# Five engine lists re-ordered over later landings of four weight pieces

## The chip, the cores and the metric

The kernel runs on one core of a Trainium2 chip. A core has a matrix engine (PE in the profile; its weight loads are shown apart as PEld), a vector engine (DVE), an activation engine (ACT), a general engine (POOL) and a queue engine (SP); 16 DMA engines move data between the core's memory and the device's memory. The metric is the time of one execution in microseconds of device time. Before the change the median of three runs is 207.43 us, the lowest 206.64 and the highest 209.45.

## The reference

```python
# x: 8 batches, 8 heads, 512 tokens, 64 wide; state: 8, 8, 32, 64
scores  = x @ state^T / 8;  a  = softmax(scores);   xread = a @ state
scores2 = state @ x^T / 8;  a2 = softmax(scores2);  sread = a2 @ x
y = concat([xread, sread], axis=2)   -> (8 * 544, 512), heads side by side
h = y @ w_in                          # 512 x 2048
g = s * relu(h) ** 2 + b
out = g @ w_out                       # 2048 x 512, float32
```

## The kernel before

**The work.** Batch by batch, the scores of x against the state are computed transposed (`T`), exponentiated on ACT (`E`) and divided by their sums (`a4`). The state is multiplied into the first weight ahead of time: `M[b, c]` is state of batch b times column chunk c of w_in, so that the first layer is `h = M^T a4`. ACT takes relu out of PSUM into `g`, DVE squares it. The second layer for batches 1 to 7 works with sums of blocks (`pd` from g, `u` from w_out; seven products in place of eight), batch 0 with plain products. The state's own rows (`sr`) go through both layers last.

**The lists.** Every piece of work is an `op` with a number, given in the order in which the Python code makes them. `TURNS` (lines 17 to 74) holds, for each of the five engines, the order in which it issues its ops; it also decides which engine does an op that two engines could do. `Plan.order` walks through these lists with a table of estimated durations. Two things come out of its estimates: which of a tag's buffers an op's output gets, and how many filler matmuls (`fill`, on the zero tile `warm`, 256 columns) are put on PE ahead of an op that, by the estimate, would find PE idle before 20 us. A filler is an instruction like any other: once it is in the list, PE runs it whether or not it would have had to wait. The constants `lands` of an op give the time at which a DMA is taken to have landed; `dma_free["sw"]` is the time at which POOL's DMA queue is taken to begin.

**The start.** SP issues the eight fp32 pieces first: ops 0 to 3 are batch 0 of x (`x0_load`, lines 446 to 453), ops 4 to 7 the four 128-row pieces k = 0 to 3 of the first column chunk of w_in (`wf_load`, lines 482 to 489). ACT or DVE casts them to fp16: ops 22 to 25 for x, 26 to 29 for w_in. POOL loads the rest with the cast done by the DMA, in the order wi 2 (op 15), wi 3 (17), wi 1 (13), wo 0 (14), x of batch 1 (18), wo 1, 2, 3 (16, 19, 20), x of batch 2 (21), each 512 KB.

For batch 0 the ops that follow are: transposes of x on PE (33, 35, 37, 39), copied to `xT` by 34, 36, 38, 40; scores of the two head groups (41, 42), their exponentials (43, 44), their sums on PE (45, 46), logarithm (47, 50), exponential of its negative (48, 51) and product (49, 52). `M[0, 0]` is op 58 on PE, which reads all four cast pieces; 59 and 60 copy its halves out of PSUM. Ops 76, 83 and 67 make `M[0, 2]`, `M[0, 3]` and `M[0, 1]` from POOL's pieces wi 2, wi 3 and wi 1. These, like every score and M op, work on tiles of 64 x 32 of the array ("tiled"); the others use all of it ("full"). The first layer of batch 0 is ops 90, 91, 94, 95, 98, 99, 102, 103 (two matmuls each) and 106, 109, 112, 115 (four each): 32 matmuls of 512 columns. Op 123 is the first product of the second layer, and reads wo 0. Later ops named below: 698 and 820 load x of batches 6 and 7 on POOL's queue; 818, 819 and 940, 941 are the DMA transposes of them on SP's queue (`att_xT_dma`, line 712), 714 the one of batch 5's quotient (line 937), 821 batch 6's scores on PE.

Every matmul is issued by the helper at line 338, every copy and cast by that at line 429.

Of the kernel before, what the change touches and what calls it, by code (L numbers as in the profile page):

```python
# [15 lines left out]

TURNS = {
    "PE": """
        33 31 35 41 37 39 45 42 58 46 94 76 90 95 91 109 83 106 112 67 115 98 102-103 99 123 127 124 135 128
        136-137 56 125 138 131 197 195 132-133 129 126 130 199 79 143 139-140 151 141 152 142 134 203 153  # L20
        144 154-155 145 202 146 156 159-160 157 161 158 162 86 118 171 175 167 172 253 173 176 174 121 147
        177 247 178 244 168 61 169 250 148 70 235 232 149-150 64 81 170 163 241 238 164 183-184 165 340 73
        1061 185-186 166 179-180 343-344 181 268 182 277-278 269-271 279 272 280 273-274 281-282 275 361 349
        1066 283 352 355 358 287 284 288-289 455 88 364 290-292 296 293-294 297-298 370 299-303 305 464 706
        704 306 315 307-310 367 316-318 311-312 577 580 586 319-321 325 322 326-327 458 460 1071 328-332 462
        699 582 385-388 477 389 394 390 395 486 471 480 391 396 489 392 397-398 474 399-400 1076 401 404-405
        492 406-408 413 409-411 414-416 602 417 599 418-420 422-424 708 702 584 425-429 432 483 442-443 433
        444-445 434-435 611 436-437 446 614 447-449 438-439 605 608 596 507-511 516 512 517 724 518-519
        513-514 520-522 721 526 523 527-529 593 530-533 535-541 821 1086 1081 542 544-549 554-555 550-551
        942 945 949 556 564 557 565-569 558 570-571 733 736 559-561 718 638-639 730 629 640 630-634 727 641  # L30
        635-636 642-643 830 826 951 644-645 648-650 715 651 855 657 652-655 658-663 666-667 664 668-672
        676-677 673 678 1096 1091 858 679-683 686 828 947 824 751 687 752 688 753 689 754 690 837 755
        691-693 849 756 846 757 760-766 758 843 767 964 770-774 779 775 780-781 776-777 782-783 840 852
        784-785 788 786 789-793 798 794-795 967 799-804 808-809 805 810-811 979 812-814 973 976 873 815
        874-875 1106 876-877 961 882-883 878-879 884-885 880 886 1111 892 970 887-888 893-895 889 1101
        896-899 901-903 958 904-907 910 908 911-917 1116 920 930-932 921 933 1136 1131 934-936 922 937 1126
        923-926 994 927 995-1001 1003 1121 1004-1008 1013-1015 1009-1010 1016-1020 1022-1027 1031-1032
        1028-1029 1033-1037 1041 1038 1042-1046 1051 1047-1048 1052-1058 1153-1160 1162-1169 1172-1179
        1181-1188 1190-1197 1200-1207 1210-1217
    """,  # L40
    "ACT": """
        36 25 43 38 47 28 48 44 50-51 96 92 84 110 107 113 69 116 100 104 201 200 80 207-208 204-205 119 254
        248 245 63 251 71 236 233 82 66 242 239 342 341 75 345-346 362 350 353 356 359 457 456 89 365 371
        465 705 707 368 578-579 581 459 461 463 701 700 478 583 487 481 472 490 493 475 603 600 703 484 585
# [3 lines left out]
    """,  # L48
    "DVE": """
        22 30 23 34 32 24 27 26 40 29 59 53 49 60 52 77-78 85 1062 93 68 111 55 97 101 57 198 196 105 114  # L50
        108 117 11 209 226 206 10 228 87 220-221 120 122 216 187 189 217 219 62 246 249 230 72 335 255 252
        234 237 65 256-257 74 240 262 243 193 218 191 347 263-264 1067 1072 1063 229 224 1068 276 258-259
        265 260 225 222 354 266 285 360 267 295 227 357 261 366 304 467-468 223 469 313 587 351 231 376 323
        1073 1082 377 363 372 333 369 379 382 589 1077 373 380 590 374 591 393 378 383 402 491 375 482 479
        412 1078 421 498 381 476 430 711 384 494 712-713 473 499 604 450 485 440 488 601 504 495-496 607
        1087 598 515 505 501 610 502 524 616 500 534 613 595 497 543 1088 620 1083 503 552 621 626 506 617
        572 723 833 618 562 834 738 835 954 623-624 637 729 646 1097 619 622 627 735 720 656 628 1092 625
        955 665 732 717 726 674 745 1093 1098 684 739 956 748 740 742-743 749 694 851 741 839 746 759 744
# [5 lines left out]
    """,  # L64
    "POOL": """
        12 15 17 13-14 18 16 19-21 212 210 214 339 194 454 576 314 334 188 698 403 192 820 286 431 451 441
        190 525 324 1080 553 573 1065 1085 1100 1070 1095 769 685 1090 647 1075 695 797 563 675 939 929 919
        817 807 891
    """,
    "SP": """  # L70
        0-3 5 4 6-9 54 338 211 337 213 215 452 336 453 348 466 574-575 697 696 470 588 1064 592 710 818-819
        1079 714 940-941 1074 832 953 1089 1069 836 1094 1099 1084 957 1050 1060 1012 1171 1040 1199 1209
        1219
    """,
}

# [13 lines left out]
class Plan:  # L90
# [34 lines left out]
    def op(self, engs, fn, rd=(), wr=(), mode=None, dma=None, since=0.0, into=(), lands=None, mms=0):  # L125
        wr_all = [*wr, *((u,) for u in into)]
        o = Op(len(self.ops), engs, fn, rd, wr_all, mode, dma, since, lands, mms)
        for key in rd:
            o.before.update(self.wrote[key])
        for key in wr:  # L130
            o.before.update(self.wrote[key])
            o.before.update(self.read[key])
        for key in rd:
            self.read[key].append(o)
        for key in wr:
            self.wrote[key] = [o]
# [14 lines left out]
    def order(self, fill):  # L151
        free = {"PE": 2.88, "ACT": 2.4, "DVE": 1.3, "POOL": 0.5, "SP": 0.6}
        queue = {e: self.turns(e)[::-1] for e in free}
        assert sum(map(len, queue.values())) == len(self.ops)
        dma_free = {"sw": 8.6, "hw": 0.0}
        big, flying, weights = 0.0, [], []
        landed = {"sw": [], "hw": []}
        slot_free = {t: [0.0] * len(s) for t, s in self.slots.items()}
# [24 lines left out]
        while any(queue.values()):  # L183
# [27 lines left out]
            if e == "PE":  # L211
# [7 lines left out]
                if t < 20 and idle > 0.11 and spare:  # L219
                    tag, i = spare[0]  # L220
# [79 lines left out]
def kernel(  # L300
# [137 lines left out]
    def xf_ap(i):  # L438
        return plan.slots["u"][i // 2].bitcast(FP32).rearrange(
            "p (h f) -> p h f", h=4  # L440
        )[:, 2 * (i % 2) : 2 * (i % 2) + 2]

    def x0_heads(i):
        return slice(4 * (i % 2) + i // 2, 4 * (i % 2) + 4, 2)

    def x0_load(i):
        op(
            {"SP": 0.5},
            lambda e: nc.sync.dma_start(xf_ap(i), x0_v[:, x0_heads(i)]),  # L449
            wr=[K(("xf", i))],  # L450
            dma=("hw", 0.75),
            lands=(3.75, 4.7, 5.95, 6.25)[i],
        )

    def x0_cast(i):
# [35 lines left out]
    def wf_cast(k):  # L491
# [82 lines left out]
    for i in range(4):  # L574
        x0_load(i)
    for k in range(NKM):
        wf_load(k)
# [789 lines left out]
    for k in range(NKM):  # L1367
# [89 lines left out]
```

## Time and profile before

| what | value |
|---|---|
| median of the runs | 207.43 us (206.64 to 209.45) |
| the profiled execution, its own time | 207.94 us |
| its span, first to last instruction | 206.2 us |
| PE busy | 199.4 us, 97% of the span |
| DVE, ACT, POOL busy | 163.5, 111.9, 35.9 us |
| filler matmuls in PE's list | 49 of 256 columns, 4 of 512 |
| granted PE clock, mean | 1.00 |

Between the span and the execution's own time lie 1.7 us outside the program's instructions. A matmul's recorded duration overlaps the next one's: the pace is read from the starts of consecutive matmuls, or from a group's start and the start of what follows. A row of the timeline gives start, duration, engine, line, operation, output and inputs by tile name, shape and count, with the idle time before it and what ended it in brackets.

### The profile page before, as it was taken

Reading aid. Unit: us, or ns where it says so; the run is one execution under the profiler, and the core shown is the slowest. Engines: PE = TensorE matmul, PEld = TensorE weight load, DVE = VectorE, ACT = ScalarE, POOL = GpSimd, SP = SyncE. Lnnn points to the kernel's source line nnn. Section 1 sums busy time; section 2 is a strip of 40 time slices with the busy share of each in tenths; the row PEclk is TensorE's granted clock in tenths of the full one; section 3 lists DMA queues with packets and bytes.
Section 4 is the critical chain, followed back from the end, with each engine's and each line's share of the span. In section 5 each row is a group of like instructions: output and inputs, shape, how many; then the busy total and the mean of one; then the engine's idle time right before and its main releaser. Section 6 shows DMA issues by size and latency. Waiting matters only on the chain.

```text
span 206.2 us, 4764 instructions
## 1 busy us (share of the span) xinstructions
PE 199.4 (97%) x1979; PEld 134.1 (65%) x1979; DVE 163.5 (79%) x329; ACT 111.9 (54%) x156; POOL 35.9 (17%) x58
## 2 busy tenths in 40 slices
PE   7699999999999999999999999999999999999992
PEld 4454454434757665766677766866777688888881
DVE  3375677799898899859998899898839869878882
ACT  2468854698587998555736667427552473221000
POOL 0850002000210103411304120004153000035000
PEclk9999999999999999999999999999999999999999
DMA  6999999999898957999963452003062100017063
GB/s 180 248 212 214 202 206 134 156 196 166 151 153 151 153 121 150 202 155 156 224 150 105 102 118 51 0 10 68 0 205 99 57 0 2 5 51 254 3 207 99
DMA packets 47302, 26.36 MB, mean 128 GB/s; under 512 B 31408, under 2 KB 44976, under 8 KB 47280
## 3 DMA queue, kind: packets, MB, share of 16 engines
q0 software_dynamic: 13216, 14.68, 36.3%
q1 hardware_dynamic: 33776, 11.28, 31.1%
q8 instruction: 15, 0.25, 0.5%
q10 hardware_dynamic: 288, 0.10, 0.2%
q14 instruction: 7, 0.06, 0.1%
HBM read 17.33 MB, written 8.91 MB: 127 GB/s over the span
## 4 chain that ended last, share of the span: by engine, by line
PE 90%; DMA 5%; DVE 2%; SPq 1%; issue 0%; ACT 0%; DVEq 0%
PE o L338 50%; PE pair L338 40%; DMA u<-in_x_dram 3%; DMA out_dram<-osb 2%; DVE osb L1293 1%; SPq L449 1%; DVE g L1025 0%; DVE osb L1304 0%; ACT xn L429 0%; DVE pd L1116 0%; DVEq L1293 0%
## 5 line engine op out<-in xcount | busy, mean ns | idle before, releaser
L1019 ACT ACTIVATE g<-pair 128x1024 f16<-128x1024 f32 x64 | 63.5, 1028 | 43.3 <-PE pair L338 43.0
L338 PE MATMUL pair<-a,M 128*128 128x512 f16 x256 | 63.3, 379 | 0.0
L338 PEld LDWEIGHTS <-pd 128*128 128x128 f16 x480 | 46.6, 98 | 11.2 <-issue 2.0
L338 PEld LDWEIGHTS <-g 128*128 128x128 f16 x424 | 40.7, 98 | 17.1 <-issue 2.5
L1025 DVE TENSOR_TENSOR g<-g 128x1024 f16<-128x1024 f16 x64 | 42.3, 683 | 3.8 <-ACT g L1019 3.8
L338 PE MATMUL o<-u,pd 128*128 128x256 f16 x360 | 44.7, 273 | 0.1
L338 PE MATMUL o<-wo,g 128*128 128x256 f16 (+1 forms) x272 | 41.7, 286 | 0.0
L338 PEld LDWEIGHTS <-M 128*128 128x128 f16 x256 | 24.4, 98 | 22.2 <-issue 1.2
L1196 POOL DMA_DIRECT2D out_dram<-osb x28 | 19.5, 766 | 102.9 <-DVE osb L1304 48.0
L1293 DVE SCALAR_TENSOR_TENSOR osb<-o,s,bias_bc 128x512 f32<-128x512 f32 (+1 forms) x32 | 22.9, 715 | 13.2 <-PE o L338 9.3
L429 ACT CAST M<-pair 128x1024 f16<-128x1024 f32 x22 | 21.6, 1015 | 6.0 <-PE pair L338 6.0
L1304 DVE SCALAR_TENSOR_TENSOR osb<-o,s,osb 128x512 f32<-128x512 f32 (+1 forms) x24 | 17.1, 714 | 5.4 <-PE o L338 5.1
L1105 DVE TENSOR_TENSOR pd<-g 128x1024 f16<-128x1024 f16 (+1 forms) x32 | 20.4, 649 | 0.0
L338 PE MATMUL o<-wo,pd 128*128 128x256 f16 x120 | 17.9, 273 | 0.0
L338 PE MATMUL o<-u,g 128*128 128x256 f16 x120 | 17.5, 273 | 0.0
L1113 DVE TENSOR_TENSOR pd<-g,pd 128x512 f16<-128x512 f16 (+1 forms) x32 | 12.7, 401 | 0.1
L1116 DVE TENSOR_TENSOR pd<-g,pd 128x512 f16<-128x512 f16 (+1 forms) x32 | 12.5, 399 | 0.0
L805 ACT ACTIVATE E<-pair 128x512 f16<-128x512 f32 x16 | 9.5, 596 | 4.7 <-DVE g L1025 3.1
L338 PE MATMUL o<-warm 128*128 128x256 f16 (+1 forms) x53 | 10.1, 325 | 1.2 <-DVE few L403 1.2
L1066 ACT ACTIVATE g<-pair 128x256 f16<-128x256 f32 x16 | 5.5, 383 | 10.5 <-PE pair L338 10.5
L973 POOL COPY srd<-srdT 128x128 f16<-128x128 f16 x8 | 6.5, 988 | 21.4 <-DMA srdT<-sr 21.4
L338 PE MATMUL pair<-wo,g 128*128 128x512 f16 x32 | 10.2, 380 | 0.0
(71 smaller groups left out, 141.1 us busy)
## 6 DMA issues: line engine op xcount, KB each, us to landing
out_dram<-osb POOLq DMA_DIRECT2D x28, 256.0 KB, 3.4
xn<-in_x_dram POOLq DMA_DIRECT2D x7, 512.0 KB, 7.4
wo<-in_moe_w_out_dram POOLq DMA_DIRECT2D x4, 512.0 KB, 18.4
wi<-in_moe_w_in_dram POOLq DMA_DIRECT2D x3, 512.0 KB, 9.9
u<-in_x_dram SPq DMA_DIRECT2D x4, 256.0 KB, 4.2
u<-in_moe_w_in_dram SPq DMA_DIRECT2D x4, 256.0 KB, 7.4
out_dram<-osb SPq DMA_DIRECT2D x4, 256.0 KB, 2.6
out_dram<-osb SPq DMA_DIRECT2D x4, 128.0 KB, 2.3
```

The lines of the kernel that those rows point to most:

```text
L338: return nc.tensor.matmul(out, lhsT, rhs, start=start, stop=stop, tile_position=tp, is_transpose=is_transpose, skip_group_check=True,)
L429: (nc.scalar.copy if e == "ACT" else nc.vector.tensor_copy)(dst, src)
L805: nc.scalar.activation(T(E[b])[:, g, :].rearrange("p (m t) -> p m t", m=2), T(u)[:, :, hS * g : hS * g + hS], AF.Exp, scale=scale, accum_o ...
L973: lambda e: nc.gpsimd.tensor_copy(srd[:, :, :, b], srdT[:, b]),
L1019: lambda e, u=u, part=part: nc.scalar.activation(part(), T(u), AF.Relu),
L1025: lambda e, part=part: nc.vector.tensor_mul(part(), part(), part()),
L1105: nc.vector.tensor_tensor(view()[:, :, 0:2], blocks(b, j)[:, :, 1:2, :].to_broadcast((P, 2, 2, n)), blocks(b, j)[:, :, 0:4:3, :], ALU.subt ...
L1113: nc.vector.tensor_tensor(view()[:, :, 2], blocks(b, j)[:, :, 3], view()[:, :, 0], ALU.subtract)
L1116: nc.vector.tensor_tensor(view()[:, :, 3], blocks(b, j)[:, :, 2], view()[:, :, 2], ALU.subtract)
L1196: lambda e: eng(e).dma_start(dst, src()),
L1293: lambda e: nc.vector.scalar_tensor_tensor(t_view(u), o_view(bank), s_bc, bias(h), ALU.mult, ALU.add),
L1304: lambda e: nc.vector.scalar_tensor_tensor(t_view(u), o_view(bank), s_bc, t_view(u), ALU.mult, ALU.add),
```

## The change

Three sets of constants in the estimates are replaced: the landings of x's four fp32 pieces, those of w_in's four, the beginning of POOL's queue, and the landing of a state piece (op 54). With these, new lists are put in for all five engines. In SP's list w_in's pieces are issued in the order k = 2, 0, 1, 3; before it was 1, 0, 2, 3. No op is added or taken away, and none computes anything else. Fifteen ops change between ACT and DVE. The fillers, which `Plan.order` works out anew, become 62 in place of 49: before the first matmul of the first layer 50 in place of 45, from there to op 123 twelve in place of four. The table of durations and the code of every op stay as they are.

```diff
     "PE": """
-        33 31 35 41 37 39 45 42 58 46 94 76 90 95 91 109 83 106 112 67 115 98 102-103 99 123 127 124 135 128
+        33 31 35 37 39 41-42 45-46 58 90 94 76 95 91 106 83 109 112 67 115 98 102 99 103 123 127 135 128 136
...
     "ACT": """
-        36 25 43 38 47 28 48 44 50-51 96 92 84 110 107 113 69 116 100 104 201 200 80 207-208 204-205 119 254
+        23-25 43-44 47 29 50 48 51 77 96 92 84 107 110 113 116 100 104 201 200 207-208 204-205 119 248 245
...
     "DVE": """
-        22 30 23 34 32 24 27 26 40 29 59 53 49 60 52 77-78 85 1062 93 68 111 55 97 101 57 198 196 105 114
+        22 30 34 36 38 32 40 28 26-27 59 53 49 60 52 78 85 10 68-69 93 55 97 57 101 196 198 108 111 105 11
...
     "POOL": """
-        12 15 17 13-14 18 16 19-21 212 210 214 339 194 454 576 314 334 188 698 403 192 820 286 431 451 441
-        190 525 324 1080 553 573 1065 1085 1100 1070 1095 769 685 1090 647 1075 695 797 563 675 939 929 919
-        817 807 891
+        12 15 17 13-14 18 16 19-21 339 214 212 210 194 454 576 314 190 334 820 286 403 188 698 324 441 1075
+        553 1090 431 451 1065 525 563 573 675 1080 695 1100 797 1085 1070 1095 647 685 807 817 192 891 939
+        929 769 919
     "SP": """
-        0-3 5 4 6-9 54 338 211 337 213 215 452 336 453 348 466 574-575 697 696 470 588 1064 592 710 818-819
-        1079 714 940-941 1074 832 953 1089 1069 836 1094 1099 1084 957 1050 1060 1012 1171 1040 1199 1209
-        1219
+        0-3 6 4-5 7-9 54 338 211 337 213 336 215 452-453 348 466 574-575 697 696 470 588 1064 592 710 941
+        714 940 819 818 1074 1069 832 1089 1079 953 1084 836 1094 957 1099 1040 1012 1060 1050 1171 1199
+        1209 1219
...
-        dma_free = {"sw": 8.6, "hw": 0.0}
+        dma_free = {"sw": 10.3, "hw": 0.0}
...
-            lands=(3.75, 4.7, 5.95, 6.25)[i],
+            lands=(3.8, 4.75, 5.9, 6.9)[i],
...
-            lands=(7.0, 7.7, 8.45, 9.2)[k],
+            lands=(8.3, 8.0, 9.0, 9.6)[k],
...
-        lands=16.6,
+        lands=18.0,
```

More of the change, by code (lines that the diff above doesn't have):

```diff
@@ L18 @@
     "PE": """
-        33 31 35 41 37 39 45 42 58 46 94 76 90 95 91 109 83 106 112 67 115 98 102-103 99 123 127 124 135 128
[L20 to L38, printed above, removed]
+        33 31 35 37 39 41-42 45-46 58 90 94 76 95 91 106 83 109 112 67 115 98 102 99 103 123 127 135 128 136
@@ new lines @@
+        124 56 131-132 129 137 195 197 125 130 138 133-134 199 79 126 151 143 139 144 147 140 203 141-142
+        148 155 145 156 202 146 149 157 159-162 86 118 175-176 158 171 247 172 177 173 121 150 178 244 174
+        253 163 61 250 152 70 232 235 153-154 81 64 164-165 241 238 167-169 166 170 179 340 73 1061 180
+        183-185 181 186 343-344 277-279 182 280 268-271 281 272 282 273-275 283 349 352 284 1066 358 361 287
+        355 288 296 455 88 289-290 364 291-292 297 293 298-299 370 294 300-303 704 706 464 305-309 315 310
@@ new lines @@
+        367 311 316 312 317 580 586 577 318-320 325-326 321 327 458 460 1071 322 328-332 699 582 462 385-389
+        394-395 390 396 489 474 391 397 392 492 480 398-400 471 401 486 404 413-414 405 1076 415 406-409 477
+        410 599 416 411 602 417-418 422-423 419-420 424-429 708 584 702 432 442-446 433 611 483 434 447-448
+        596 435-436 449 605 593 437-439 614 516 608 507-513 517-521 514 522-523 721 724 526-533 535-539 821
+        1081 1086 540-542 544-550 554-555 551 556 942 949 945 564 557 565-570 558-559 730 560-561 571 733
@@ new lines @@
+        736 629 727 630-632 638-639 718 640-642 633-636 643-644 830 826 951 645 648-655 715 657-660 666 661
+        667-668 858 662-664 855 669-672 676 673 1096 1091 828 824 947 677-679 686 680 687-689 852 690 681
+        691-692 682 693 683 846 843 760 751 761 752-754 762-763 755-758 764-765 849 770-771 837 766-767
+        772-776 840 779 777 780 967 788 781-784 789 785-786 790-795 798-799 964 808-813 979 800 976 961
+        814-815 801-802 973 1101 970 803 873 1111 804-805 958 874-880 882-885 1106 886-889 892-898 901-903
@@ L39 @@
+        899 904 1116 905 910-911 906 912 907-908 913-917 920-924 930 925 931-935 1121 936 1136 937 1131
+        926-927 1126 994-997 1003 998-999 1004 1000-1001 1005-1010 1013-1017 1022 1018 1023 1019-1020
+        1024-1028 1031-1032 1029 1033-1038 1041-1047 1051-1052 1048 1053-1058 1153-1160 1162-1169 1172-1179
         1181-1188 1190-1197 1200-1207 1210-1217
@@ L41 @@
     "ACT": """
-        36 25 43 38 47 28 48 44 50-51 96 92 84 110 107 113 69 116 100 104 201 200 80 207-208 204-205 119 254
-        248 245 63 251 71 236 233 82 66 242 239 342 341 75 345-346 362 350 353 356 359 457 456 89 365 371
-        465 705 707 368 578-579 581 459 461 463 701 700 478 583 487 481 472 490 493 475 603 600 703 484 585
[3 rows of a table removed]
+        23-25 43-44 47 29 50 48 51 77 96 92 84 107 110 113 116 100 104 201 200 207-208 204-205 119 248 245
+        254 62 251 71 233 236 82 65 242 66 239 342 341 74-75 345-346 350 353 359 362 356 457 456 89 365 371
@@ L48 @@
+        705 707 465 368 581 579 578 459 461 463 700-701 490 583 493 475 472 487 478 481 600 603 585 709 703
[3 rows of a table added]
     """,
     "DVE": """
-        22 30 23 34 32 24 27 26 40 29 59 53 49 60 52 77-78 85 1062 93 68 111 55 97 101 57 198 196 105 114
-        108 117 11 209 226 206 10 228 87 220-221 120 122 216 187 189 217 219 62 246 249 230 72 335 255 252
-        234 237 65 256-257 74 240 262 243 193 218 191 347 263-264 1067 1072 1063 229 224 1068 276 258-259
-        265 260 225 222 354 266 285 360 267 295 227 357 261 366 304 467-468 223 469 313 587 351 231 376 323
@@ L54 @@
[L54 to L58, printed above, removed]
[5 rows of a table removed]
+        22 30 34 36 38 32 40 28 26-27 59 53 49 60 52 78 85 10 68-69 93 55 97 57 101 196 198 108 111 105 11
@@ new lines @@
+        80 117 209 114 87 206 224 120 228 122 189 187 63 255 216 72 249 335 252 220 230 237 246 243 221 234
+        265 240 262 256 223 193 191 257 347 1062 225 276 1067 1063 259 226 266 260 217-218 229 1068 285 263
+        227 231 261 1072 258 357 222 267 360 354 363 264 351 295 219 304 467-469 313 587 373 366 1073 323
+        379 369 333 374 372 380 382 589 376 590-591 393 377 1077 402 476 494 381 488 375 383 1078 1082 473
[3 rows of a table added]
+        1097 628 1098 1093 674 739 729 948 684 694 732 956 740 743 748 759 749 860 745-746 768 778 845 741
@@ L64 @@
+        842 848 787 750 796 744 864 747 854 969 839 966 861 851 865 981 866 816 857 870 862 806 985 867-869
[4 rows of a table added]
     """,
     "POOL": """
-        12 15 17 13-14 18 16 19-21 212 210 214 339 194 454 576 314 334 188 698 403 192 820 286 431 451 441
-        190 525 324 1080 553 573 1065 1085 1100 1070 1095 769 685 1090 647 1075 695 797 563 675 939 929 919
-        817 807 891
+        12 15 17 13-14 18 16 19-21 339 214 212 210 194 454 576 314 190 334 820 286 403 188 698 324 441 1075
+        553 1090 431 451 1065 525 563 573 675 1080 695 1100 797 1085 1070 1095 647 685 807 817 192 891 939
```

18 rows, old and new, of the table TURNS are left out of this document.

## The prediction

> **What bounds the kernel now.** I read the page's first two parts, then the chain that ended last, then PE's busy time in two stretches, and only then single rows.
>
> ```profile
> span 206.2 us, 4764 instructions
> ```
>
> ```profile
> PE 199.4 (97%) x1979; PEld 134.1 (65%) x1979; DVE 163.5 (79%) x329; ACT 111.9 (54%) x156; POOL 35.9 (17%) x58
> ...
> PEclk9999999999999999999999999999999999999999
> ```
>
> ```profile
> 2.27 6.36 DMA u<-in_x_dram
> ```
>
> ```profile
> 14.32:23.09 8.77, 8.77 (x62) 3.50 (x61) 5.75 (x11) 7.01 (x9) 0.89 (x1) 1.00 1.29 209
> 23.09:202.20 179.11, 179.02 (x1827) 123.32 (x1825) 151.02 (x295) 98.35 (x135) 28.42 (x44) 1.00 0.64 118
> ```
>
> PE is the bound, at the full clock throughout. The chain begins with a transfer: the fourth fp32 piece of x (op 3), issued at 2.27 us, lands at 8.6. From the first matmul of the first layer, at 14.32, PE is never idle for long: 8.77 us of 8.77 busy, then 179.02 of 179.11 (stretch, length, then busy time and count for PE, PEld, DVE, ACT, POOL). So a change of order can gain only by starting that first matmul sooner, by dropping something PE executes, or in the last few microseconds. The lists' last part (ops 1153 to 1217 on PE, the last four DMAs on SP) is the same in both, so the end gives nothing. It can lose wherever it puts in work or a wait.
>
> **The change part by part.**
>
> *The fp32 pieces.* Where the four pieces of w_in land is read from the casts that start as they come:
>
> ```profile
> 9.90 0.49 DVE L429 CAST wi<-u 128x512 f16<-128x512 f32 x1 [3.43 <-DMA u<-in_moe_w_in_dram]
> ...
> 11.86 0.77 DVE L429 CAST wi<-u 128x512 f16<-128x512 f32 x1 [0.39 <-DMA u<-in_moe_w_in_dram]
> 13.18 0.69 DVE L429 CAST M<-pair 128x512 f16<-128x512 f32 x1 [0.55 <-PE pair L338]
> ...
> 13.85 0.42 DVE L852 TENSOR_TENSOR a<-E,a 128x512 f16<-128x512 f16 x1
> ```
>
> ```profile
> 11.25 0.62 ACT L429 CAST wi<-u 128x512 f16<-128x512 f32 x1 [0.35 <-DMA u<-in_moe_w_in_dram]
> 11.77 0.59 ACT L846 ACTIVATE a<-o 128x512 f16<-128x512 f32 x1
> 12.26 0.59 ACT L805 ACTIVATE E<-pair 128x512 f16<-128x512 f32 x1
> ```
>
> The first is cast at 9.90, the last at 11.86: the third at 11.25, so 0.6 to 0.7 us apart, in the order of issue. The new lists assume 8.0 to 9.6, some 2 us earlier than this execution shows. Issuing k = 2, 0, 1, 3 only permutes which piece has which place; k = 3 stays last, and op 58 needs all four. Cost: 0. The Trainium skill speaks against reading an order into this: "DMA: Bandwidth & Descriptors", section "Queues, rings and completion order", says that completion is not first-in, first-out per issuing engine, since each of the 16 DMA engines runs its own ring. By that page piece 2 could come last; DVE, which now casts 2, 0, 1 in that order, would hold all three behind it, 3 x 0.5 us from 11.86 to 13.4, and the sum would be 0.8 us longer; the trace, with its spacing in order of issue, gives 0.
>
> *The first 14 us.* ACT now casts the second to fourth piece of x; the fourth still at 8.64, as it lands. PE then does op 39 and only then the scores 41, which before had run early; so the first exponential goes from 9.17 to about 10.1. The second goes the other way, from 12.26 to about 10.8, because ACT no longer puts a copy, a logarithm, a cast and an exponential ahead of it. By rows of 0.5 to 0.6 us each ACT then does op 47 to 11.8, the cast of piece 3 (landed 11.84) from 11.9 to 12.4, 50 to 12.9, 48 to 13.4, 51 to 13.9. Before, 48 was done at 12.36. That hides: its user, the product 49, stands on DVE behind op 59, the copy of M that ran from 13.18 in the trace (49 at 13.85). Op 58 waits for the last cast: on DVE that took until 12.63, on ACT it ends near 12.5, so 58 is 0.1 us earlier, and 59, 49 and the first first-layer matmul with it: 14.2 instead of 14.32. The twelve fillers now between 58 and that matmul take 12 x 0.109 = 1.3 us from about 12.9, also 14.2: they just fit. I take -0.1; bounds -0.2 (all the casts' gain) and +0.3 (ACT's cast kept back by op 47, then the fillers wait behind 58).
>
> *From the first first-layer matmul to op 123*, which starts at 23.09. Here is PE's list as it ran:
>
> ```profile
> 14.32 0.59 PE L338 MATMUL pair<-a,M 128*128 128x512 f16 x2
> 14.75 0.27 PE L338 MATMUL o<-warm 128*128 128x256 f16 x1
> 14.95 0.41 PE L338 MATMUL o<-wi,stT 64*32 64x512 f16 x8
> 15.29 1.47 PE L338 MATMUL pair<-a,M 128*128 128x512 f16 x6
> 16.60 0.27 PE L338 MATMUL o<-warm 128*128 128x256 f16 x1
> 16.71 1.03 PE L338 MATMUL pair<-a,M 128*128 128x512 f16 x4
> 17.67 0.41 PE L338 MATMUL o<-wi,stT 64*32 64x512 f16 x8
> 18.01 1.90 PE L338 MATMUL pair<-a,M 128*128 128x512 f16 x8
> 19.75 0.38 PE L338 MATMUL o<-warm 128*128 128x256 f16 x2
> 20.06 0.41 PE L338 MATMUL o<-wi,stT 64*32 64x512 f16 x8
> 20.40 2.85 PE L338 MATMUL pair<-a,M 128*128 128x512 f16 x12
> 23.09 0.81 PE L338 MATMUL o<-wo,g 128*128 128x512 f16 x3
> ```
>
> A 512-column matmul costs (18.01 to 19.75, eight of them) 0.216; a filler (14.75 to 14.95 with the change into a tiled block, 16.60 to 16.71 alone) 0.11; a tiled block 0.34 (14.95 to 15.29, 17.67 to 18.01, 20.06 to 20.40) and some 0.09 to get into it. Before: 32 x 0.216 + 3 x 0.43 + 4 x 0.109 = 6.91 + 1.29 + 0.44 = 8.64, of the 8.77 seen; 0.13 is waiting. After: the same 32 and the same three blocks, but twelve fillers, two ahead of op 76, seven ahead of 83, three ahead of 67: 6.91 + 1.29 + 1.31 = 9.51. That is 0.74 more if all the waiting goes, 0.87 if none does. Do the eight new fillers replace waiting? They stand in front of blocks that need POOL's pieces wi 2, wi 3 and wi 1:
>
> ```profile
> L505 POOL DMA_DIRECT2D wi<-in_moe_w_in_dram x3: 760/766/911, 6.1 to 7.8; - x3
> ...
> DMA to landing us min/median/max: 8.2/9.9/12.1
> ```
>
> Issued at 6.1, 7.0 and 7.8, they land (shortest, middle, longest) at 14.3, 16.9 and 19.9, and PE came to the blocks at 14.95, 17.67 and 20.06: 0.6, 0.7 and 0.2 us after. PE waited for none, and POOL's list is the same here, so fillers only push. After: op 123 at 14.2 + 9.5 = 23.7, against 23.09. Sum so far **+0.6**; bounds 0 (fillers all cover a wait) and +1.2 (0.87 + 0.3).
>
> *From 23 to 202 us.* The matmuls are the same in number and shape, and PE runs them one behind the other. PE's list goes from full to tiled or column tiles 18 times instead of 19: -0.1. One stall of before was this:
>
> ```profile
> 152.27 0.75 DVE L1293 SCALAR_TENSOR_TENSOR osb<-o,s,bias_bc 128x512 f32<-128x512 f32 x1 [3.52 <-DMA out_dram<-osb]
> ```
>
> ```profile
> 152.38 2.38 PE L338 MATMUL o<-u,pd 128*128 128x256 f16 x18
> ```
>
> DVE waited for an output store to land; the 18 matmuls took 2.38 where 17 x 0.109 + 0.27 = 2.12 would do: 0.25 us of PE. The new POOL list puts the stores in another order; this stall may go. The new orders can as well bring stalls that no row shows. What speaks for few: the re-ordered DMAs mostly keep microseconds between landing and use. The tightest I find is batch 6's x. Its load (698) now follows batch 7's (820) on POOL, and SP issues its transposes behind 714, 940 and one another:
>
> ```profile
> 85.46 4.45 SPq L712 DMA_TRANSPOSE xT<-xn  x2
> ...
> 97.49 1.24 SPq L937 DMA_TRANSPOSE a<-aN  x1
> 98.83 2.95 SPq L712 DMA_TRANSPOSE xT<-xn  x2
> ```
>
> ```profile
> 111.02 0.43 PE L338 MATMUL pair<-xT,stT 64*32 64x256 f16 x16
> ```
>
> ```profile
> DMA to landing us min/median/max: 3.3/5.3/12.0
> ```
>
> Before, they were issued from 85.46, 25 us ahead of their use at 111.02. Now: 714 from 97.5 + 0.6, then 940, 819, 818 at about 1.4 us each (98.83 and 2.95 for two), so the last is issued near 102.2 and lands, by the median of the transposes (5.3), at 107.5: 4 us ahead of 111.6. On SP the batch-1 and batch-2 read transposes queue behind them, for which PE's column blocks wait near 112; also in time by 3 us. I take 0 for this stretch: the bounds are -0.35 (both gains, no new wait) and +2.6 (the longest transpose, 12.0 after 102.2, is 114.2).
>
> **Sum.** -0.1 + 0.74 + 0 = +0.6 us. The profiled execution took 207.94 (span 206.2 and 1.7 around it); it would be 208.6. It stands 0.5 over the median 207.43, so the median goes to about 208.1.
>
> **The rivals.**
>
> *The fillers cost nothing* (not slower). If the fp32 pieces land 2 us sooner than here, as the new constants say, while POOL's come at the same times, the first layer starts sooner and PE really waits before 76, 83 and 67. It decides from the point where POOL's pieces are about 0.9 us later against the first matmul than here: then the old list waits too (its slack at 67 is 0.2) and the new fillers lie inside the waits. What is left is -0.1 and -0.25: 207.1. For it: landings differ between executions, and the runs spread by 2.8 us. Against it: three positive slacks in the one execution shown.
>
> *A new wait late in the lists* (slower). Batch 6's transposes, as above: with 12.0 us to landing PE stands at 821 for 2.6 us, and 208.1 becomes 210.7. To pass 2% it needs a landing 3.5 us later than the need, or a second such wait, an output store that holds DVE as at 152.27 but for as long as DVE itself waited, 3.5 us: then 211.6 and more. Against it: before has one stall in 179 us.
>
> *The order of the pieces does not hold* (the page's rule): 208.1 + 0.8 = 208.9.
>
> **How the numbers follow.** Forecast 0.58, own range 207.6 to 208.8; fillers free 0.20 (206.9 to 207.5); late wait 0.18 (209 to 212, under half of it over 211.6); pieces out of order 0.03; anything else 0.01. The range leaves out the lower edge of the second and the upper part of the third: 206.9 to 210.6. Two per cent, about what a measurement of this kernel can tell from no change, is 4.1 us: slower than 211.6 has 0.08, all from the late wait; faster than 203.3 would need PE's start four microseconds sooner, 0.02; the rest 0.90.
>
> **What would show it.** After: op 58 near 12.4 and the first first-layer matmul near 14.2; a row of seven fillers ahead of the second tiled block, none of the three blocks waiting; the first `o<-wo,g` near 23.7; PE busy without a gap to about 202.7; no long wait of DVE at 152; landings of x's transposes by 108. Wrong would be: a first-layer start by 13, since then the landings moved; PE standing for over a microsecond behind 23 us; or `o<-wo,g` under 23.2.

## The result, and the profile after

After the change the median is 208.46 us (207.59 to 211.38, 20 runs); before, on the same chip, it is 207.18 us (206.46 to 209.45, 20 runs). The ratio is 1.006, with a 95% interval of 1.0044 to 1.0077: the change costs about 1.3 us, less than the 2% that count as a difference here, but more than its own uncertainty. Two of the runs of after, 211.12 and 211.38, lie more than 1.5% above its fastest and are left out of the ratio. The forecast was 208.1, reached as 0.64 us over a median of 207.43; the measured rise is twice that, over a median of before that is 0.25 lower.

The profiled execution of after took 209.84 us, 1.4 above its median; the one of before stood 0.76 above the 20-run median (207.94). The two profiles are therefore further apart (1.9 us) than the medians, and the terms below are sizes in these two executions. What the terms are worth on average is left to the experiments.

From the page of after: the span, the busy times, the clock over the span, and the chain that ended last, as shares by engine.

```profile
span 208.0 us, 4778 instructions
...
PE 200.9 (97%) x1992; PEld 135.1 (65%) x1992; DVE 165.7 (80%) x330; ACT 110.1 (53%) x155; POOL 36.9 (18%) x58
...
PEclk9999999999999999999999999999999999999999
...
PE 73%; DVE 13%; DMA 7%; issue 2%; ACT 2%; SPq 0%; DVEq 0%
```

PE has thirteen matmuls more (the fillers) and is still the bound at the full clock. To see where the time went, PE's busy time is taken in the two stretches that the prediction used: from the first matmul of the first layer to op 123, and from there to PE's end (columns: stretch, length, then busy time and count for PE, PEld, DVE, ACT and POOL, clock, DMA share, GB/s).

```profile
13.08:22.73 9.65, 9.65 (x70) 4.31 (x68) 4.80 (x10) 7.05 (x9) 1.77 (x2) 1.00 1.28 207
22.73:204.24 181.51, 179.78 (x1827) 123.56 (x1825) 154.01 (x298) 95.99 (x134) 28.50 (x43) 1.00 0.65 116
```

For before, the prediction's second stretch stopped at 202.20; up to the end of PE's last matmul, as taken here for after, it is

```profile
23.09:202.42 179.33, 179.23 (x1827) 123.32 (x1825) 151.02 (x295) 98.35 (x135) 28.42 (x44) 1.00 0.64 118
```

Against before the first-layer start is 1.24 us earlier (13.08 against 14.32), the way to op 123 is 0.88 longer (9.65 against 8.77), and the rest is 2.2 longer (181.51 against 179.33): PE idles 1.7 us there, where it idled 0.1.

**The start.** The last of the four casts of w_in began at 11.86 in before. In after it has moved to ACT:

```profile
8.94 0.42 DVE L428 CAST wi<-u 128x512 f16<-128x512 f32 x1
...
9.52 0.50 DVE L428 CAST wi<-u 128x512 f16<-128x512 f32 x1 [0.16 <-DMA u<-in_moe_w_in_dram]
...
10.18 0.72 DVE L428 CAST wi<-u 128x512 f16<-128x512 f32 x1 [0.16 <-DMA u<-in_moe_w_in_dram]
```

```profile
10.77 0.62 ACT L428 CAST wi<-u 128x512 f16<-128x512 f32 x1
```

It begins at 10.77, 1.09 us sooner, because the pieces landed sooner in this execution. From that cast to the first-layer start it was 14.32 - 11.86 = 2.46 us; it is 13.08 - 10.77 = 2.31, so only 0.15 us of this pair's difference can be the lists' doing. Over the fourteen profiles of this study the last fp32 piece lands between 9.6 and 11.8 us, with either version. Nor do they bear out the 0.15 as a general gain. From that landing to the first-layer start the old start takes 2.36 to 2.51 us in five profiles and 3.11 in a sixth; the new one, with the pieces issued as in after, takes 2.33 to 2.34 in four and 2.77 to 2.84 in three, where ACT comes to its cast some 0.5 us after the piece has landed.

**The fillers.** PE's timeline in after, from the first layer to op 123:

```profile
13.08 1.03 PE L337 MATMUL pair<-a,M 128*128 128x512 f16 x4
13.95 0.38 PE L337 MATMUL o<-warm 128*128 128x256 f16 x2
14.26 0.41 PE L337 MATMUL o<-wi,stT 64*32 64x512 f16 x8
14.60 1.90 PE L337 MATMUL pair<-a,M 128*128 128x512 f16 x8
16.34 0.93 PE L337 MATMUL o<-warm 128*128 128x256 f16 x7
17.20 0.41 PE L337 MATMUL o<-wi,stT 64*32 64x512 f16 x8
17.54 1.90 PE L337 MATMUL pair<-a,M 128*128 128x512 f16 x8
19.27 0.49 PE L337 MATMUL o<-warm 128*128 128x256 f16 x3
19.70 0.41 PE L337 MATMUL o<-wi,stT 64*32 64x512 f16 x8
20.04 2.86 PE L337 MATMUL pair<-a,M 128*128 128x512 f16 x12
22.73 0.59 PE L337 MATMUL o<-wo,g 128*128 128x512 f16 x2
```

Two, seven and three fillers, one behind the other, and no wait ahead of a tiled block. The seven take 17.20 - 16.34 = 0.86 us.

**Behind 22 us.** PE's waits between 23 and 200 us in after (engine, what waited, for whom: total, times, longest), and the rows of PE's timeline at the first:

```profile
PE pair L337 <- DVE osb L1235: 0.6, 1, 0.6
PE o L337 <- DVE osb L1292: 0.6, 1, 0.6
PE o L337 <- DVE osb L1303: 0.5, 2, 0.4
```

```profile
50.12 0.59 PE L337 MATMUL pair<-E,bones 128*128 128x512 f16 x2
50.55 0.82 PE L337 MATMUL o<-wo,g 128*128 128x256 f16 x6
51.98 0.38 PE L337 MATMUL pair<-wo,g 128*128 128x512 f16 x1 [0.61 <-DVE osb L1235]
```

The matmul at 51.98 is op 182. Five matmuls at the pace of 0.11 from 50.55, and a sixth, end at 51.21, so 0.77 us are lost. Op 182 is the last product of one half of a two-bank `pair` tile of batch 0; op 193, on DVE at line 1235, reads the other half into `osb`. The old list had 182 ahead of 193 in the program, the new one has it behind 186, 343, 344 and 277 to 279, and 193 comes first. The planner's table keeps the halves apart, but the wait that is emitted covers the tile: PE stands until DVE has read the half that 182 doesn't touch.

The other two come from a transfer. SP's transpose of batch 5's `E` into `aT` (op 710), and POOL's load of batch 6's x beside it, then the sum on DVE that waited for it (all of after):

```profile
85.64 1.29 SPq L894 DMA_TRANSPOSE aT<-E  x1
```

```profile
85.87 0.91 POOL L469 DMA_DIRECT2D xn<-in_x_dram  x1
```

```profile
aT<-E SPq DMA_TRANSPOSE x1, 10.8
```

```profile
96.46 1.22 DVE L916 TENSOR_REDUCE r<-aT 128x32 f32<-128x1024 f16 x1 [2.74 <-DMA aT<-E]
```

```profile
102.73 0.38 PE L337 MATMUL o<-wo,g 128*128 128x256 f16 x2 [0.59 <-DVE osb L1292]
...
104.33 1.91 PE L337 MATMUL o<-wo,g 128*128 128x256 f16 x16 [0.35 <-DVE osb L1303]
```

Issue to landing is 10.8 us. The same transpose in before (its issues, by operation: KB, median us to landing, here of one):

```profile
aT<-E SPq DMA_TRANSPOSE x1, 3.2
```

There it was issued at 84.1 and landed at 87.3, beside two output stores; the next load of x went out only at 86.5. In after the load of 512 KB follows the transpose by 0.23 us. DVE loses 2.74 us and hands part of it on to PE, 0.59 at 102.73 and 0.35 at 104.33, and some 0.4 between 115 and 118. With the 0.77 that is 2.1 of the 2.2 us. The Trainium skill, "DMA: Bandwidth & Descriptors", section "Issuing engines are not separate DMA queues", says that transfers started by different engines run on the same 16 DMA engines and interleave. By that rule the two meet here although one is SP's and one POOL's; the trace agrees, with 10.8 against 3.2 us.

### The profile page after: what moved, and what is told of

Its sections match the earlier page's. It is cut to its first block, busy times and chain, and to the rows that moved or that the text cites. A ratio compares the mean times of both kernels' runs of the same rounds, so it can differ in the third digit from the quotient of the medians.

```text
span 208.0 us, 4778 instructions
## 1 busy us (share of the span) xinstructions
PE 200.9 (97%) x1992; PEld 135.1 (65%) x1992; DVE 165.7 (80%) x330; ACT 110.1 (53%) x155; POOL 36.9 (18%) x58
## 4 chain that ended last, share of the span: by engine, by line
PE 73%; DVE 13%; DMA 7%; issue 2%; ACT 2%; SPq 0%; DVEq 0%
PE o L337 41%; PE pair L337 32%; DMA aT<-E 5%; DVE g L1024 4%; DVE pd L1104 2%; DMA u<-in_x_dram 2%; DVE osb L1292 2%; DVE osb L1303 1%; ACT M L428 1%; DVE r L916 1%; DVE aN L928 1%; DVE pd L1112 1%; DVE pd L1115 1%; ACT g L1018 0%; DVE u L1141 0%
## 5 line engine op out<-in xcount | busy, mean ns | idle before, releaser
L337 PE MATMUL o<-u,pd 128*128 128x256 f16 x360 | 44.2, 273 | 0.0
L1024 DVE TENSOR_TENSOR g<-g 128x1024 f16<-128x1024 f16 x64 | 42.9, 685 | 0.9 <-ACT g L1018 0.9
L337 PE MATMUL o<-wo,g 128*128 128x256 f16 (+1 forms) x272 | 39.1, 285 | 0.9 <-DVE osb L1292 0.6
L428 ACT CAST M<-pair 128x1024 f16<-128x1024 f32 x19 | 18.6, 1015 | 6.3 <-PE pair L337 6.3
L337 PE MATMUL o<-wo,pd 128*128 128x256 f16 x120 | 18.5, 273 | 0.0
L337 PE MATMUL o<-u,g 128*128 128x256 f16 x120 | 16.9, 273 | 0.2 <-DVE osb L1303 0.2
L337 PE MATMUL pair<-wo,g 128*128 128x512 f16 x32 | 9.7, 381 | 0.6 <-DVE osb L1235 0.6
L337 PE MATMUL o<-warm 128*128 128x256 f16 (+1 forms) x48 | 9.2, 327 | 1.2 <-DVE few L402 1.2
L337 PEld LDWEIGHTS <-warm 128*128 128x128 f16 x66 | 6.6, 107 | 4.7 <-issue 1.6
```

What stands on the lines that cost most here:

```text
L337: return nc.tensor.matmul(out, lhsT, rhs, start=start, stop=stop, tile_position=tp, is_transpose=is_transpose, skip_group_check=True,)
L428: (nc.scalar.copy if e == "ACT" else nc.vector.tensor_copy)(dst, src)
L1024: lambda e, part=part: nc.vector.tensor_mul(part(), part(), part()),
```

## The experiments

The questions: do the fillers cost their time on PE (called F in the expectations), does the late part of the lists lose (W in the first four expectations, L in the later ones), is it the wait for the shared tile or the late transpose, and does the order of the pieces count. Every kernel computes the whole output. Ratios are to the kernel before on the same chip, with 95% intervals. The medians of before in the three series are 207.41 (first four runs), 207.49 (next four) and 207.25 (last four); 0.001 of the ratio is 0.21 us. The ratios are not the quotients of the medians (208.12 by 207.41 would be 1.0034 in the first run below, where the ratio is 1.0029); a difference given in us beside a ratio is taken from ratios.

In the runs on fillers, `Plan.order` takes their number ahead of some ops from a table in place of the estimate:

```diff
+    FILLS = {...}          # op: fillers ahead of it
...
-                if t < 20 and idle > 0.11 and spare:
+                if o.n in self.FILLS and spare:
+                    tag, i = spare[0]
+                    out += [(fill, self.slots[tag][i])] * self.FILLS[o.n]
+                elif t < 20 and idle > 0.11 and spare:
```

**After with the four fillers of before**

```diff
+    FILLS = {76: 1, 83: 1, 67: 2}
```

> The changed kernel with the fillers ahead of ops 76, 83 and 67 set to 1, 1 and 2 in place of 2, 7 and 3: eight filler matmuls fewer, nothing else changed. Theory F (the eight extra fillers push PE): 8 x 0.109 = 0.87 us less, 207.6 us. Theory W (the loss comes from waits behind 23 us, above all the transpose of batch 5's E that lands 10.8 us after its issue beside the load of batch 6's x; the fillers lie inside waits): 208.3 to 208.5.

Measured: median 208.12 us, ratio 1.0029 [1.0006, 1.0053], against 1.006 with twelve: 0.64 us less. The time lies between what F and W had expected. Its profile, first layer to op 123:

```profile
13.38:22.32 8.94, 8.84 (x62) 3.60 (x60) 4.80 (x10) 6.94 (x9) 1.76 (x2) 1.00 1.28 209
```

The eight fillers fewer make this stretch 0.71 us shorter (9.65 to 8.94). With them gone PE waits 0.10 us ahead of the third tiled block, for POOL's piece wi 1.

**Before with the twelve fillers of after**

```diff
+    FILLS = {76: 2, 109: 0, 83: 7, 67: 3}
```

> The kernel before with 2, 7 and 3 fillers ahead of ops 76, 83 and 67 and none ahead of 109, in place of 1, 0, 2 and 1: eight filler matmuls more. F: 207.18 + 0.87 = 208.0 us, op 123 starting 0.7 to 0.9 us later against the first first-layer matmul. W: 207.2 to 207.4.

Measured: 208.41 us, 1.0037 [1.0011, 1.0063]: 0.77 us slower than before, from fillers alone. First layer to op 123 took 9.64 us, as in after. In this execution POOL's pieces wi 2 and wi 3 had landed by 13.4 and 16.0, 0.6 and 1.4 us ahead of the blocks at 13.99 and 17.36; without the seven fillers, 0.86 us, PE would have come to the second at 16.5, still behind the landing. The third block is another matter. With the four fillers of before PE comes to it 5.74 us after the first first-layer matmul (20.06 - 14.32), here at 18.99; wi 1 landed at 19.67. In this execution some 0.7 of the 0.87 us of the eight fillers lay in a wait for wi 1 that the shorter list would have had.

**The new lists to op 123 with the old ones behind, and the reverse.** Each engine's list is the ops that run before op 123 from one version, then all others from the other version.

> The new lists up to op 123 (the 88 or so ops that run before 23 us), the old lists behind it, the new constants, so the same fillers as in the changed kernel. F: 207.18 + 0.6 to 0.8 = 207.8 to 208.0 us. W: 207.0 to 207.3, as nothing of the late part is new.

> The old lists up to op 123 with the old constants and fillers, the new lists behind it. F: 207.2 to 207.6 us. W: 208.2 or more, with the transpose of batch 5's E again landing about 10 us after its issue, beside the load of batch 6's x.

Measured: new then old 207.99 us, 1.0017 [0.9993, 1.0041]; old then new 207.90, 1.0013 [0.9991, 1.0034]. Neither alone is told from no change, and together they make 0.6 of the 1.25 us; intervals of half a microsecond each way leave room for that. The second is under the 208.2 that theory W had expected. The profiles say more. With the old start and its four fillers, in the second kernel, the way to op 123 took nearly as long as with twelve, since two of POOL's pieces landed late against the first layer:

```profile
13.02:22.48 9.46, 8.90 (x62) 3.67 (x60) 5.21 (x10) 7.01 (x9) 2.05 (x3) 1.00 1.26 206
```

```profile
13.93 0.41 PE L337 MATMUL o<-wi,stT 64*32 64x512 f16 x8 [0.21 <-DMA wi<-in_moe_w_in_dram]
...
19.46 0.41 PE L337 MATMUL o<-wi,stT 64*32 64x512 f16 x8 [0.35 <-DMA wi<-in_moe_w_in_dram]
```

With the old late part, PE takes 179.32 us from op 123 to its end, as in before. With the new one the wait at line 1235 is there again:

```profile
51.73 0.38 PE L337 MATMUL pair<-wo,g 128*128 128x512 f16 x1 [0.61 <-DVE osb L1235]
```

The transpose's delay was milder in that execution: it landed 6.8 us after issue, and PE waited nowhere between 101 and 118 us.

**After with op 182 put back ahead of 186**

```diff
-        183-185 181 186 343-344 277-279 182 280 268-271
+        183-185 181-182 186 343-344 277-280 268-271
```

> The changed kernel with one matmul, op 182 (last of its bank, in the tile that op 193 on DVE reads), moved from behind 277 to 279 to ahead of 186, so that it stands before op 193 in the program. Theory L1 (the 0.77 us stall at 51 us, seen in the changed kernel and in both experiments with its late part, is PE waiting for DVE to have read the other half of the same tile): no stall there, 0.77 us less from op 123 to PE's end and in the median, about 207.7 us. Rival (DVE is simply late there, and the stall moves to the next reader): the same time as the changed kernel, 208.4.

Measured: 207.87 us, 1.0008 [0.9984, 1.0033]. PE's timeline at the place:

```profile
50.52 0.59 PE L337 MATMUL pair<-E,bones 128*128 128x512 f16 x2
50.96 2.02 PE L337 MATMUL o<-wo,g 128*128 128x256 f16 x17
```

Seventeen matmuls run on without a gap. So the wait was the order of 182 against 193, and nothing that 182 itself needs. The late transpose is still there (9.8 us to landing), and PE still loses 0.30, 0.15 and 0.23 us between 102 and 117 us, counted from start to start against the run with both waits off, below.

**After with batch 6's load held back until the transpose has landed**

```diff
     def x_load(b, rd=()):
+            if b == 6:
+                nc.gpsimd.tensor_copy(gate, T(aT[5])[:, 0, 0, 0:2])
             nc.gpsimd.dma_start(...)
...
+    plan.ops[698].before.add(plan.ops[710])
```

> The changed kernel, where POOL reads two numbers of batch 5's transposed E before it issues the load of batch 6's x, so that the load begins behind the transpose's landing. Theory L2 (the load issued 0.3 us after the transpose holds it for 7 to 11 us): the transpose lands 3 to 4 us after its issue, and the waits of PE between 101 and 118 us, 1.9 us in the profile of the changed kernel and 0.3 in that of the first experiment, go; 0.2 to 1.3 us less in the median. Rival (these waits come from DVE's order alone): the transpose lands early and PE waits all the same.

Measured: 208.25 us, 1.0024 [0.9998, 1.005]. The transpose, POOL's rows and PE's timeline in this run:

```profile
aT<-E SPq DMA_TRANSPOSE x1, 4.9
```

```profile
90.88 0.18 POOL L469 COPY gate<-aT 128x2 f16<-128x2 f16 x1 [4.89 <-DMA aT<-E]
91.51 0.91 POOL L470 DMA_DIRECT2D xn<-in_x_dram  x1 [0.45 <-PE o L337]
```

```profile
102.21 0.38 PE L337 MATMUL o<-wo,g 128*128 128x256 f16 x2
102.43 1.03 PE L337 MATMUL pair<-a,M 128*128 128x512 f16 x4
103.29 2.89 PE L337 MATMUL o<-wo,g 128*128 128x256 f16 x25
```

The load, and one output store that POOL issues behind it, go out 5.6 us later than in after, the transpose lands in 4.9 us, and the products wait no longer at 102 to 104. So the load (with that store) was the cause of the delay. The wait at 51 us is left in this kernel.

**Before with no fillers there at all**

```diff
+    FILLS = {76: 0, 109: 0, 67: 0}
```

> The kernel before with no filler ahead of ops 76, 109 and 67 (four fewer). Theory F (a filler there costs its 0.109 us where the piece that POOL loads has landed): 0.2 to 0.44 us less than before, 207.0. Rival (PE waits for the piece instead): 207.2 to 207.4, no difference.

Measured: 208.45 us, 1.002 [0.9986, 1.0054]. Four of the twelve runs lie at 206.75 to 206.98, eight at 208.17 to 209.43, and none between. The profiled one, 206.96, is of the lower four. It took 8.82 us to op 123, against 8.77 with the fillers: the time that the fillers had taken became, for the most part, a wait for POOL's piece wi 1.

```profile
19.31 0.41 PE L342 MATMUL o<-wi,stT 64*32 64x512 f16 x8 [0.35 <-DMA wi<-in_moe_w_in_dram]
```

F, which expected less time, misses. The eight slower runs have no profile; why there are two groups stays open. What can be said is that four fillers fewer brought no gain here, and that in the profiled execution they would have lain in a wait.

**After with the pieces issued in the order of before**

```diff
-        0-3 6 4-5 7-9 54
+        0-3 5 4 6-9 54
```

> The changed kernel with w_in's four fp32 pieces issued in the old order 1, 0, 2, 3, all else as changed; DVE still casts 2, 0, 1 in this order. By the prediction the order has no price as the last piece stays last: DVE's casts of 0 and 1 come up to 0.5 us later, behind that of 2, and the last of the four casts ends up to 0.5 us later than in the changed kernel: 0 to +0.5 us, 208.4 to 208.9. Rival (the order is what the change gains by): +1 us or more.

Measured: 208.96 us, 1.0065 [1.0043, 1.0088], against 1.006 for after: no price on the order that these times can tell. The profile has a small one: DVE casts piece 2 first, which here lands third, and the first layer begins 2.56 us after the last landing, against 2.33 in after.

**After with both late waits off** (op 182 and batch 6's load, the two edits above together).

> The changed kernel with both edits of the second series: op 182 ahead of 186, and the load of batch 6's x behind the landing of batch 5's transpose. Theory L (both late waits cost, the fillers the rest): from op 123 to PE's end 179.1 us, about what the old lists take (179.3), and a median 0.2 to 0.4% over before, which is the eight fillers. Rival (something else in the late lists costs as well): 180 us and more from op 123 to the end.

Measured: 207.62 us, 1.0007 [0.9988, 1.0025]. From op 123 to PE's end:

```profile
22.85:202.10 179.25, 179.24 (x1827) 123.45 (x1825) 154.33 (x298) 95.96 (x134) 29.00 (x44) 1.00 0.62 117
```

PE idles 0.01 us where it idled 1.7. With the wait at line 1235 alone (batch 6's load held back) the same way takes 179.88 us, with the transpose's delay alone (182 moved up) 179.90, with both, in after, 181.51. Against after's 1.006, 1.1 us are gone, and the time is below the 0.2 to 0.4% over before that was expected. The edit of 182 alone had come to 1.0008, so the times do not tell what the transpose costs on average beside it; the profiles, counted from start to start between 100 and 120 us against this run, show 0.5 to 1.6 us of PE's time lost where the landing took 9.7 to 10.8 us, and none where it took 6.8.

**The same with the four fillers of before**

```diff
+    FILLS = {76: 1, 83: 1, 67: 2}
```

> The same with 1, 1 and 2 fillers ahead of 76, 83 and 67 in place of 2, 7 and 3. If late waits and fillers are the whole of the loss: equal to before within 0.2%, or up to 0.4 us below it. Rival (fewer fillers bring something else, as in the run of before with four fewer, where runs fell into two groups 2 us apart): two groups again, median over 208.

Measured: 206.94 us, 0.9981 [0.9957, 1.0005].

```profile
13.11:21.89 8.78, 8.78 (x63) 3.51 (x60) 4.80 (x10) 6.87 (x9) 1.75 (x2) 1.00 1.28 209
```

The stretch is back at 8.78 us, and 0.0026 of the ratio, 0.54 us, has gone with the eight fillers. Taking the two late waits out took 0.0053 off the ratio and the fillers 0.0026, from 1.0060 to 0.9981: these changes are enough to remove the whole loss.

**Before with its four fillers moved to an earlier place**

```diff
+    FILLS = {39: 4, 76: 0, 109: 0, 67: 0}
```

> The kernel before with the four fillers of ops 76, 109 and 67 put ahead of op 39 instead, where PE waits for x: as many instructions on PE as before, none of them between the first first-layer matmul and op 123. Theory F: 0.2 to 0.4 us less than before, 207.0. Rival for the two groups of the run with four fewer (they come from PE having fewer instructions, which shifts where its code is fetched): one group here. If the two groups come from the missing fillers themselves: two groups here too.

Measured: 206.96 us, 0.9977 [0.9956, 0.9999], at the time that F expected and barely better than before; one interval in some twelve may end just short of 1 by chance. Twelve of thirteen runs lie at 206.36 to 207.15. The thirteenth, at 208.21, is the profiled one, and shows PE waiting for POOL's pieces, longest for these two:

```profile
13.87 0.41 PE L342 MATMUL o<-wi,stT 64*32 64x512 f16 x8 [0.61 <-DMA wi<-in_moe_w_in_dram]
...
18.18 0.41 PE L342 MATMUL o<-wi,stT 64*32 64x512 f16 x8 [1.64 <-DMA wi<-in_moe_w_in_dram]
```

Piece wi 3 landed 4.3 us behind wi 2, where 2.6 is usual. A late piece of POOL's is thus one way to a run over 208; whether it is what made the slower group of the run with no fillers isn't shown. The twelve runs in one group fit the rival that the expectation names (two groups come from fewer instructions on PE), but no run here shows its reason.

**The old lists to op 123 with the new late part, both waits off** (the split lists from above, with the edits of op 182 and of batch 6's load).

> The old lists up to op 123 with the old fillers, the new ones behind it with both edits. Theory L: from op 123 to PE's end 179.1 us, 0.2 us less than the old lists, which keep their own stall of 0.25 us at 152: before to 0.2% under it. Rival (the new late lists lose by more than the two waits): 0.1 to 0.3% over before.

Measured: 207.15 us, 0.9985 [0.9964, 1.0007]. From op 123 to PE's end:

```profile
22.39:201.49 179.10, 179.10 (x1827) 123.53 (x1825) 154.00 (x297) 96.23 (x134) 28.61 (x44) 1.00 0.63 118
```

Mended, the new late part takes 179.10 us without a stall, against 179.33 for the old one. The way to op 123, with four fillers, took 9.66 us in this execution, 0.76 of it idle ahead of tiled blocks, since wi 2 and wi 1 landed late against the first layer (wi 1 6.60 us after its first matmul). No kernel here is shown to beat before by more than its interval, but for the moved fillers, whose interval ends at 0.9999.

## Why the prediction was right, and where it was wrong

The time came out 0.36 us over the forecast, and it is slower than before, as forecast. That the total came so near is in part luck: the median of before that it starts from was 0.25 us too high, and the rise was 1.28 us in place of 0.64. The mechanism that it put its weight on, fillers that push PE, is there; a second one, larger, it put at nothing.

*The fp32 pieces*: order at no cost, right within what the times can tell. In all fourteen profiles the four pieces land in the order of issue, 0.6 to 1.0 us apart (in after at 8.79, 9.50, 10.16 and 10.75), and the old order in the new lists measures the same. The Trainium skill, "DMA: Bandwidth & Descriptors", section "Queues, rings and completion order", says that completion need not follow issue; none of these profiles shows it, and they can't exclude it.

*The first 14 us*: forecast -0.1, and -0.15 in the one pair of profiles, from the last cast's start to the first-layer start. Over all profiles no gain is left: counted from the last landing, the new start (the run with the old order of pieces included) and the old one both average 2.54 us, and three of the new ones show ACT's cast kept back by what stands ahead of it, which the prediction had as its bound of +0.3. The start at 14.2 was over a microsecond off, since it took the landings of one execution for fixed: they move by 2.2 us between executions. A start near 13 was named as the sign that the landings had moved, and so it was.

*From the first first-layer matmul to op 123*: forecast 9.51, seen 9.65. The 0.13 us that the sum called waiting was none: without any wait four fillers take 8.77 and 8.78 us, twelve take 9.65, so the eight are 0.87 on PE. In the time of the kernel they measured 0.54, 0.64 and 0.77 us in three comparisons of ratios (intervals of some half a microsecond each way). The difference is what the prediction's first rival describes. With four fillers PE comes to the third block 5.74 us after the first matmul, with twelve 6.61, and what decides is where wi 1 lands on this scale. It landed at 5.53 in before, and between 5.29 and 7.86 in the others, later than 5.74 in nine of the fourteen. Where it landed at 6.40 and 6.60, kernels with four fillers took 9.46 and 9.66 us, about as long as those with twelve. In after itself it landed at 6.29: by this estimate four fillers would have waited there until 6.33, and the eight more cost some 0.3 us in that execution, not the 0.88 that the two profiles differ by. So the rival in which the fillers cost nothing is right for some executions, and wrong on average; the prediction took the slacks of one execution for all.

*From 23 to 202 us*: this is the step that failed. It was taken as 0, with a bound of +2.6, and cost 1.1 us by the ratios, 2.2 in the one profile. PE stood 1.7 us there, in waits of at most 0.6; over a microsecond was the prediction's own sign of being wrong. The stall at 152 of before is indeed gone: no output store holds DVE there. But two waits came. One, 0.77 us at 51, stands in no row of before and was not seen in the lists: a product of one half of a tile put behind the reader of the other half. It can be read off the two lists without a run, by asking of each moved PE op whether a reader of the same tile now comes before it. The other is the mechanism of the second rival, a transpose slowed by its neighbours, but on another transpose. The prediction looked at batch 6's x: its two transposes were issued at 102.95 and 104.33 and had landed by 110.1, ahead of their use at 112.26. The one that hurt is batch 5's `aT`, op 710, which did not change its place by much; what moved is POOL's load, now 0.23 us behind it. The prediction asked which transfers had moved, and should have asked also what each moved transfer now runs beside. In before such a meeting was in the quoted 12.0 us of a transpose of x, which landed at 98.8 with 12 us to spare.

Left over may be a gain of some 0.4 us (0.9981 with all three mended), but its interval reaches to 1.0005, and no gain is shown. The profiles put 0.1 to 0.2 us to the late part without its waits (179.10 to 179.24, against 179.33) and nothing steady to the start.

## What to carry to other kernels

When lists are re-ordered, look for readers as well as for inputs: a matmul that fills one half of a two-bank tile, put behind the reader of the other half, cost PE 0.77 us for data it never touched. And list, for every large load that moves, the small transfers on other queues issued within a few microseconds of it: a transpose of 3.2 us took 10.8 beside a load of 512 KB, and only the one without slack cost anything. A filler matmul that an estimate puts into a gap costs its full 0.1 us whenever the gap isn't there. Here the gap came and went with the landings, which move by 2 us between executions, so one profile can't price the fillers: set the landing against the first matmul in several, and count them as work where it comes early.

## What the runs showed of the hardware beyond what was expected

- Landings of the first transfers differ by 2.2 us between executions (last fp32 piece 9.6 to 11.8 us). POOL's 512 KB pieces that hold w_in follow one another by 2.4 to 3.2 us in most profiles; in three of fourteen one came 3.7 to 4.3 us behind the one ahead of it.
- Batch 5's transpose landed in 3.2 to 6.5 us where the next load of x went out 2.4 us behind it (the old late lists, five profiles), in 4.8 to 5.2 with the load held back until it had landed, and in 6.8 to 10.8 with the load issued 0.2 us behind it.
- PE's granted clock was 1.00 in every stretch shown, with waits of up to 1.6 us and with eight fillers fewer.
- The old kernel without the four fillers falls into two groups of runs about 2 us apart, the lower (206.75 at best) no faster than the fastest runs of before (206.52) on the same chip. The cause could not be settled.
